# One-hot rows per tile, a copy moved to ScalarE, and other steps reordered in a fused attention and mixture-of-experts kernel

## The chip, the cores and the metric

One core of a Trainium2 chip runs the whole kernel. The metric is the device time of one execution in microseconds, as the median of several runs; before the change it is 367.67 us (three runs, 366.77 to 367.95).

The engines appear in the profile as PE (TensorE, with PEld for its weight loads), DVE (VectorE), ACT (ScalarE), POOL (GpSimd) and SP (SyncE, which only issues transfers here). L12 is line 12 of the kernel before.

## The reference

Attention without softmax, with an RMS norm over each head, and then a layer of eight experts in which each token goes to one expert or to none.

```python
# q, k, v: (8, 8, 576, 64); g_norm: (64,)
kv  = np.einsum('bhsd,bhse->bhde', k, v)
out = np.einsum('bhsd,bhde->bhse', q, kv)
rms = np.sqrt(np.mean(out * out, axis=-1, keepdims=True) + 1e-06)
attn = out / rms * g_norm
x = attn.transpose(0, 2, 1, 3).reshape(4608, 512)

do = x @ w_skip > 0                        # tokens that are computed
logits = x[do] @ w_gate                    # 8 experts
e_idx = argmax(logits); p = softmax(logits)[e_idx]
y = p * (relu(x[do] @ w1[e_idx]) @ w2[e_idx])     # w1[e]: 512x1024, w2[e]: 1024x512
out = x;  out[do] = x[do] + y
```

## The kernel before

The kernel writes its instructions in an order set by hand; each engine runs its own list in that order, and semaphores join them. It has an attention part (to about 107 us) and an experts' part.

**The attention part** runs over 36 units. A unit is 256 tokens' worth of rows for four heads: `units` lists a batch, one of its two blocks of columns, and a half of the heads (`u`). Eight batches in two groups of four make 4 times 8 units and, after each group, two units that gather the rows left over (with `i` None). The main loop (`for n in range(NU + 2)`) writes one step per unit:

- `turn(n + 1)`: four TensorE transposes of q for the next unit (L460), and a ScalarE copy, `qT` (L463).
- `root(n - 1)`: ScalarE's square root of the sums of squares (L529).
- `jobs(n, "early")`, then `values(n)`: for the first two units of a batch two more transposes into the same bank (`turn_8`, L479), four products of qT with k^T v (L498; L508 for the left-over rows), and ScalarE's Square, `sq` (L514). The results go to one of two `o_ps` banks; units 30 and 33 (`THIRDS`) use the bank `sum_ps` instead. A bank is free again when `xl` of its unit is made.
- `jobs(n, "mid")`, `squares(n)` (VectorE's sums `rs`, L522), `norm(n - 1)` (reciprocal L536 and `xl`, L545), `jobs(n, "pe")`; up to step `THIRD + 1` (29) `squares` stands behind `norm`, later ahead of it.
- `finish` and `scale`: GpSimd adds up the gate logits (`lp`, `lg`) and multiplies by the norm's gains (`xb`, L615), which then goes out. `xb` is held back until VectorE's next reciprocal.

**k^T v** of the batches ahead is summed between the units' products (`state`, L383, into `sum_ps`), following the table `portions`. When a batch is done, ScalarE copies the sums to `both` (L390); VectorE copies two quarters of it across partitions into `kvd` (`other`, L394) and GpSimd two more (`own`, L395). `state_t` turns it (L400, copy L402), and `state_m` multiplies by the gate's weights (L408) with four small ScalarE copies into `kvd` (L412). `kvT_ps`, `lg_ps` and the ranks lie side by side in one bank, `g_ps`.

**The tokens' numbering** goes in three groups of 12, 10 and 14 tiles of 128 tokens (`ends`). For each group a stream of small VectorE jobs is written, 2 or 4 to a step (`PACE`): `choose` (the expert of each token, one-hot as `ohb`), `rank` (L696 to L702: running counts by matmul, on top of `top`), `number` (L713 to L728: the slot of each token, split into `hi_k` and `lo_i`, and `oha_k`, for each tile a 128x128 one-hot of its `lo_i`). After the second group `rank_experts` sorts the experts by their counts and SP reads the order; then `early` sends for the first expert's first tokens: `hits` and `bv`, 22 matmuls with `oha_k` (`put`, L924), sums (`rows`, L928), and an indirect gather on GpSimd (L917); `put_more` (L934) does the same for 64 more. `first_in` transposes those tokens (L848) at the "pe" places of steps 33 and 34.

**SP's queue** issues q, k and v (L118), each in four parts, and the stores of `xb` (L653), in the order of the steps.

**The experts' part** (from L1172 on) takes one expert after another, with TensorE's products on sums of blocks (L1252).

## Time and profile before

| | |
|---|---|
| median of three runs | 367.67 us |
| the profiled execution | 366.29 us |
| its span, first to last instruction | 364.4 us |
| TensorE busy, granted clock | 96%, 0.994 |
| 80 to 100 us: PE / DVE / ACT / POOL busy | 17.67 / 18.14 / 13.18 / 14.76 of 20 us |
| 100 to 120 us: the same | 19.23 / 17.69 / 12.27 / 12.82 of 20 us |

A profile's row has its start in us from the span's start, its length, engine, line, operation, what it writes and reads, shapes, and in brackets how long the engine was idle just before and what released it. Consecutive rows of one line are merged, with their count. Starts of successive rows on an engine tell its pace better than lengths, since the end of one operation overlaps the start of the next. Of transfers the profile gives issue and landing.

### The profile page before, as it was taken

The page shows a single profiled execution, that of the slowest core. Times are in us where ns is not written, and L with a number is a line of the kernel's source. Part 1 is how long each engine was busy: PE and PEld are TensorE (multiplying, and loading weights), DVE is VectorE, ACT ScalarE, POOL GpSimd, SP SyncE. Part 2 cuts the span into 40 slices and gives each one's busy share as a digit, 9 for nine tenths or more (in the row PEclk, how much of TensorE's full clock was granted, in tenths as well). Part 3 has the DMA queues.
Part 4 walks back from the last instruction along what each step waited for, and adds up shares of the span by engine and source line. Part 5 has one row for each costly group of instructions (what it writes and reads, how often), then busy time and mean ns, then how long its engine had stood idle before and what let it go on. Part 6 is the DMA issues. An engine that isn't in the chain of part 4 may idle for free.

```text
span 364.4 us, 9568 instructions
## 1 busy us (share of the span) xinstructions
PE 349.5 (96%) x3754; PEld 305.5 (84%) x3754; DVE 249.2 (68%) x637; ACT 145.1 (40%) x418; POOL 125.7 (34%) x205
## 2 busy tenths in 40 slices
PE   8979998999899999999999999999999999999994
PEld 4769987888779669599879978989988998989983
DVE  2545677889888563876937676786776776878831
ACT  2537775676666244244104402512421530431420
POOL 8036777677776072123041102303203203002003
PEclk9989999999999999999999999999999999999999
DMA  8999999999797369873535537455563762601001
GB/s 272 387 390 377 371 392 398 394 394 384 247 335 255 104 208 379 340 262 89 209 107 205 171 124 254 121 224 176 175 230 98 250 235 53 243 1 58 3 2 54
DMA packets 32808, 81.70 MB, mean 224 GB/s; under 512 B 3242, under 2 KB 3250, under 8 KB 32756
## 3 DMA queue, kind: packets, MB, share of 16 engines
q1 hardware_dynamic: 28944, 69.48, 53.7%
q0 software_dynamic: 3792, 11.53, 9.3%
q8 instruction: 31, 0.51, 0.5%
q14 instruction: 21, 0.17, 0.1%
q10 hardware_dynamic: 20, 0.02, 0.0%
HBM read 66.80 MB, written 14.48 MB: 223 GB/s over the span
## 4 chain that ended last, share of the span: by engine, by line
PE 79%; issue 6%; DMA 5%; DVE 5%; POOL 2%; ACT 2%; SPq 0%; POOLq 0%; DVEq 0%; ACTq 0%
PE bank L1252 46%; PE bank L1184 9%; PE o_ps L498 6%; PE sum_ps L383 4%; PE bank L1172 3%; PE q_ps L460 3%; DMA v<-in_v_dram 2%; PE bank L1153 2%; DVE xl L545 1%; DMA xg<-out_dram,src 1%; PE g_ps L859 1%; DMA xg<-out_dram,asrc 1%; PE q_ps L859 1%; PE o_ps L479 1%; DVE rs L522 1%
## 5 line engine op out<-in xcount | busy, mean ns | idle before, releaser
L1262 ACT COPY p<-bank 128x128 f32<-128x128 f32 (+6 forms) x70 | 20.8, 297 | 96.1 <-PE bank L1252 94.6
L1252 PE MATMUL bank<-xt,w 128*128 128x128 f32 (+5 forms) x336 | 55.4, 288 | 0.1
L1383 POOL DMA_INDIRECT out_dram<-xg,rows x14 | 13.9, 996 | 116.2 <-DVE xg L1380 113.0
L1252 PEld LDWEIGHTS bank<-xt,w 128*128 128x128 f32 x336 | 47.0, 190 | 1.9 <-DVE bank L1256 1.4
L615 POOL TENSOR_TENSOR xb<-xl,g_b 128x512 f32<-128x512 f32 x34 | 41.3, 1216 | 18.1 <-DVE rs L536 16.1
L1256 DVE TENSOR_TENSOR bank<-bank,p 128x128 f32<-128x128 f32 (+6 forms) x70 | 23.6, 337 | 29.7 <-PE bank L1252 28.7
L498 PE MATMUL o_ps<-kvd,qT 128*128 128x146 f32 x240 | 36.0, 293 | 1.3 <-DVE xl L545 1.0
L1252 PE MATMUL bank<-xs,s 128*128 128x128 f32 (+5 forms) x224 | 36.7, 288 | 0.0
L498 PEld LDWEIGHTS o_ps<-kvd,qT 128*128 128x128 f32 x240 | 32.1, 192 | 2.1 <-DVE xl L545 1.8
L1252 PEld LDWEIGHTS bank<-xs,s 128*128 128x128 f32 x224 | 31.1, 190 | 1.0 <-ACT p L1262 0.8
L1184 PE MATMUL bank<-w,ht 128*32 128x128 f32 (+2 forms) x424 | 29.9, 313 | 0.0
L522 DVE TENSOR_REDUCE rs<-sq 128x8 f32<-128x512 f32 x36 | 24.5, 681 | 5.4 <-ACT sq L514 5.2
L545 DVE TENSOR_TENSOR xl<-o_ps,rs 128x584 f32<-128x584 f32 x32 | 24.5, 767 | 4.3 <-DVE rs L536 0.5
L1184 PEld LDWEIGHTS bank<-w,ht 128*32 128x32 f32 (+2 forms) x424 | 18.2, 119 | 10.6 <-issue 7.2
L1252 PE MATMUL bank<-t,ht 128*128 128x256 f32 x112 | 27.0, 384 | 0.0
L1252 PE MATMUL bank<-w,ht 128*128 128x256 f32 x112 | 26.5, 380 | 0.0
L383 PE MATMUL sum_ps<-v,k 64*64 64x64 f32 x1152 | 23.5, 223 | 3.0 <-issue 2.6
L1144 POOL DMA_INDIRECT xg<-out_dram,src x14 | 14.3, 1024 | 34.8 <-DMA out_dram<-xg,rows 18.0
L514 ACT ACTIVATE sq<-o_ps 128x512 f32<-128x512 f32 x34 | 20.3, 596 | 14.1 <-PE o_ps L498 13.2
L383 PEld LDWEIGHTS sum_ps<-v,k 64*64 64x64 f32 x1152 | 19.6, 134 | 7.1 <-issue 3.9
L1252 PE MATMUL bank<-t,hs 128*128 128x256 f32 x112 | 25.3, 379 | 0.0
L1252 PEld LDWEIGHTS bank<-t,ht 128*128 128x128 f32 x112 | 20.8, 190 | 3.9 <-issue 1.2
(216 smaller groups left out, 665.2 us busy)
## 6 DMA issues: line engine op xcount, KB each, us to landing
w<-in_moe_w_dram SPq DMA_DIRECT2D x16, 2048.0 KB, 9.0
k<-in_k_dram SPq DMA_DIRECT2D x32, 288.0 KB, 6.0
v<-in_v_dram SPq DMA_DIRECT2D x32, 288.0 KB, 6.3
q<-in_q_dram SPq DMA_DIRECT2D x32, 288.0 KB, 6.2
out_dram<-xb SPq DMA_DIRECT2D x29, 256.0 KB, 6.1
out_dram<-xb POOLq DMA_DIRECT2D x7, 256.0 KB, 6.4
xg<-out_dram,src POOLq DMA_INDIRECT x16, 3.6
out_dram<-xg,rows POOLq DMA_INDIRECT x16, 6.1
```

What stands on the lines that cost most here:

```text
L383: nc.tensor.matmul(out=sum_ps[w * 64:(w + 1) * 64, a, u, :], lhsT=kt[r, 2 * u + w, c, :], rhs=vt[r, 2 * u + w, c, :], start=(c == 0), stop ...
L498: mm = nc.tensor.matmul(out=ps[:, w, 0:2 * PK].rearrange("p (r k) -> p r k", r=2)[:, :, cols], lhsT=qT[:, w, a, :], rhs=kvds[b % KVD][:, w ...
L514: nc.scalar.activation(out=sq[:, :, :, :], in_=heads(ps, G, G + 2 * D), func=ACT.Square)
L522: nc.vector.tensor_reduce(out=rs[:, :, :], in_=sq[:, :, :, :].rearrange("p x y (a d) -> p x (y a) d", a=2), axis=AX.X, op=ALU.add)
L545: nc.vector.tensor_tensor(out=xl[:, :, :, :].rearrange("p x y (a k) -> p x (y a) k", a=2), in0=ps[:, :, 0:2 * PK].rearrange("p x (h k) -> ...
L615: late.append((lambda eng: eng.tensor_tensor(out=xb[:, :, 4 * u * D:(4 * u + 4) * D].rearrange("p r (w x) -> p r w x", w=2), in0=xl[:, :, ...
L1144: nc.gpsimd.indirect_dma_start(out=x_of(xg, off, m), out_offset=None, in_=cut_rows(m)[:, :], in_offset=bass.IndirectOffsetOnAxis(ap=idx[:, ...
L1184: nc.tensor.matmul(out=yps[q * m:(q + 1) * m, 0:n], lhsT=ht(f)[:, off:off + m], rhs=w_sb[r][1][:, f, q * n:(q + 1) * n], start=(f == 0), s ...
L1252: nc.tensor.matmul(out=out, lhsT=lhsT(i), rhs=rhs(i), start=start and i == 0, stop=i == k - 1, skip_group_check=True)
L1256: nc.vector.tensor_tensor(out=to, in0=x, in1=y, op=ALU.add)
L1262: nc.scalar.copy(out=t, in_=x)
L1383: ins = nc.gpsimd.indirect_dma_start(out=cut_rows(m)[:, :], out_offset=bass.IndirectOffsetOnAxis(ap=rows[:, col:col + 1], axis=0), in_=x, ...
```

## The change

Six edits:

- `oha_k` is made one tile at a time, by a TENSOR_SCALAR that compares a two-byte row of the numbers 0 to 127 (`row128`) with that tile's `lo`, a per-partition scalar; before, one TENSOR_TENSOR on whole numbers made two tiles (or seven in the last group). `lo` comes from `hi_k` by a multiply and add, in place of a bitwise and.
- For the batches from 5 on (`ACROSS`), ScalarE makes the two copies of k^T v across partitions, one ahead of `values` and one behind it, in place of VectorE.
- `rank` moves from the place "pe" to "mid"; `state_m` of batches 4 and 6 (`RANKED`) moves to "early" of the next step.
- `rank_experts` does without three small operations: `kbase` is made once in the setup, and the order is summed straight to whole numbers.
- In `early`, the sums and both gathers (`put_rows`) move behind `squares`; the transposes of the unit after next are written ahead of them.
- The step from which `squares` stands ahead of `norm` is `THIRD + 1` in place of `THIRD + 2`.

```diff
-    row128_i = keep.tile([P, P], I32)
+    row128_i = att_pool.tile([P, P], I32, tag="sq", name="row128_i", bufs=2)
     nc.gpsimd.iota(row128_i[:, :], pattern=[[1, P]], base=0, channel_multiplier=0)
+    row128 = keep.tile([P, P], BF16)
...
+    nc.vector.tensor_copy(out=row128[:, :], in_=row128_i[:, :])
...
+    kbase = keep.tile([P, E], FP32)
+    nc.vector.scalar_tensor_tensor(out=kbase[:, :], in0=ebase[:, :], scalar=-float(E),
+                                   in1=eorder[:, :], op0=ALU.mult, op1=ALU.add)
...
         for w in range(2):
-            nc.vector.tensor_copy(out=other(b, w)[:, :, cols], in_=both[w * 64:(w + 1) * 64, :, :])
+            if b < ACROSS:
+                nc.vector.tensor_copy(out=other(b, w)[:, :, cols], in_=both[w * 64:(w + 1) * 64, :, :])
             nc.gpsimd.tensor_copy(out=own(b, w)[:, :, cols], in_=both[w * 64:(w + 1) * 64, :, :])
 
+    def state_across(b, w):
+        if b >= ACROSS:
+            nc.scalar.copy(out=other(b, w)[:, :, G:G + 2 * D], in_=boths[b][w * 64:(w + 1) * 64, :, :])
...
-        lo_i = gat_pool.tile([P, TG], I32, tag="lo_i", name="lo_i")[:, 0:nt]
-        nc.vector.tensor_single_scalar(out=lo_i, in_=s_i, scalar=127, op=ALU.bitwise_and)
-        yield
         nc.vector.tensor_single_scalar(out=hi_k[:, t0:t1], in_=s_i, scalar=7,
                                        op=ALU.arith_shift_right)
         yield
+        lo = gat_pool.tile([P, TG], FP32, tag="lo", name="lo")[:, 0:nt]
+        nc.vector.scalar_tensor_tensor(out=lo, in0=hi_k[:, t0:t1], scalar=-128.0, in1=s_i,
+                                       op0=ALU.mult, op1=ALU.add)
+        yield
         step = 2 if g < LAST else nt // 2
         for t in range(0, nt, step):
-            nc.vector.tensor_tensor(out=oha_k[:, t0 + t:t0 + t + step, :],
-                                    in0=row128_i[:, :].unsqueeze(1).to_broadcast([P, step, P]),
-                                    in1=lo_i[:, t:t + step].unsqueeze(2).to_broadcast([P, step, P]),
-                                    op=ALU.is_equal)
+            for i in range(t, t + step):
+                nc.vector.tensor_scalar(out=oha_k[:, t0 + i, :], in0=row128[:, :],
+                                        scalar1=lo[:, i:i + 1], scalar2=None, op0=ALU.is_equal)
             yield
...
-        key = count_tokens("key", gat_pool)
-        nc.vector.scalar_tensor_tensor(out=key[:, :], in0=key[:, :], scalar=float(E),
-                                       in1=eorder[:, :], op0=ALU.mult, op1=ALU.add)
+        key = gat_pool.tile([P, E], FP32, tag="key", name="key")
+        nc.vector.scalar_tensor_tensor(out=key[:, :], in0=top[:, :], scalar=float(E),
+                                       in1=kbase[:, :], op0=ALU.mult, op1=ALU.add)
...
-        nc.vector.tensor_reduce(out=order_f[:, :], in_=gt[:, :, :], axis=AX.X, op=ALU.add)
-        yield
-        nc.vector.tensor_copy(out=order_i[:, :], in_=order_f[0:1, :])
+        with nc.allow_low_precision(reason="whole numbers"):
+            nc.vector.tensor_reduce(out=order_i[:, :], in_=gt[:, :, :], axis=AX.X, op=ALU.add)
...
-            rows = gat_pool.tile([P, 2], FP32, tag="rows1", name="rows1")
-            nc.vector.tensor_reduce(out=rows[:, :], in_=ps.rearrange("p (c i) -> p c i", i=2),
-                                    axis=AX.X, op=ALU.add)
-            gather(rows[:, 0:1], P, 0)
-
-            def put_more():
+            turn(now[0] + 2)
+            turned_ahead.append(now[0] + 2)
+
+            def put_rows():
+                rows = gat_pool.tile([P, 2], FP32, tag="rows1", name="rows1")
+                nc.vector.tensor_reduce(out=rows[:, :], in_=ps.rearrange("p (c i) -> p c i", i=2),
+                                        axis=AX.X, op=ALU.add)
+                gather(rows[:, 0:1], P, 0)
                 more = g_ps[:, GB + 4:GB + 5]
...
                 gather(more, 64, P)
-            at(now[0], "pe", put_more)
+            assert now[0] > THIRD
+            at(now[0], "squared", put_rows)
...
+    RANKED = (4, 6)
...
-            at(step, "pe", lambda b=b: state_m(b))
+            for w, part in enumerate(("early", "mid")):
+                at(step, part, lambda b=b, w=w: state_across(b, w))
+            at(step + (b in RANKED), "early" if b in RANKED else "pe", lambda b=b: state_m(b))
...
-        yield lambda: rank(g)
+        yield "mid", lambda: rank(g)
...
-        if 1 <= n < NU - 1:
+        if 1 <= n < NU - 1 and n + 1 not in turned_ahead:
             turn(n + 1)
...
-        if THIRD + 2 <= n < NU:
+        if THIRD < n < NU:
             squares(n)
+        jobs(n, "squared")
         done = norm(n - 1) if 1 <= n <= NU else None
-        if n < THIRD + 2:
+        if n <= THIRD:
             squares(n)
```

What this moves, at three places. The line numbers of the changed kernel are higher by 5 to 10.

TensorE around the second ranking, before: the products of unit 24 (`kvd_161`), `state_m` of batch 6 (L408), a part of batch 7's sums (L383), then the ranking, whose first row is L696.

```order
L498 MATMUL o_ps<-kvd_161,qT 128x2x73 x4
L408 MATMUL g_ps<-gw_b,kvT 128x36 x2
L383 MATMUL sum_ps<-v,k 64x64 x16
L696 MATMUL g_ps<-top,ident 128x88
L699 LDWEIGHTS ut
```

The same place in the changed kernel, and, behind the ranking's rows, what follows up to unit 25's products:

```order
L508 MATMUL o_ps<-kvd_163,qT 128x2x73 x4
L706 MATMUL g_ps<-top,ident 128x88
L709 LDWEIGHTS ut
...
L712 MATMUL g_ps<-ohb,ones 128x8
L388 MATMUL sum_ps<-v,k 64x64 x16
L470 MATMUL q_ps<-ident,q 128x2x64 x4
L418 MATMUL g_ps<-gw_b,kvT 128x36 x2
L508 MATMUL o_ps<-kvd_163,qT 128x2x73 x4
```

The ranking now follows the products directly, and `state_m` (now L418) stands behind the transposes of unit 26's q (L470), ahead of unit 25's products.

TensorE around the placing for the first gather, before: unit 29's products, unit 31's transposes, unit 30 (`sum_ps`), the 22 placing matmuls (L924), and the one that waits for their sums (L934).

```order
L498 MATMUL o_ps<-kvd_164,qT 128x2x73 x4
L460 MATMUL q_ps<-ident,q 128x2x64 x4
L479 MATMUL sum_ps<-ident,q 128x128 x2
L498 MATMUL sum_ps<-kvd_167,qT 128x2x73 x4
L924 LDWEIGHTS oha_k
...
L934 MATMUL g_ps<-rows_2044,again_64_243 128x1
L460 MATMUL q_ps<-ident,q 128x2x64 x4
```

In the changed kernel:

```order
L508 MATMUL o_ps<-kvd_166,qT 128x2x73 x4
L932 LDWEIGHTS oha_k
...
L470 MATMUL q_ps<-ident,q 128x2x64 x4
L944 MATMUL g_ps<-rows_2039,again_64_247 128x1
L489 MATMUL sum_ps<-ident,q 128x128 x2
L508 MATMUL sum_ps<-kvd_169,qT 128x2x73 x4
L470 MATMUL q_ps<-ident,q 128x2x64 x4
```

The placing comes one unit sooner, unit 31's transposes stand between it and the matmul on its sums (now L944), and unit 30's products stand behind that matmul.

VectorE between the sums of unit 27 and the first gather's rows, before: each group of L536, L545, L522 is the reciprocal and `xl` of one unit and the sums of the next.

```order
L522 TENSOR_REDUCE rs<-sq 128x8
L728 TENSOR_TENSOR oha_k<-row_i,lo_i 128x256 x3
L899 TENSOR_TENSOR ohc_1975<-hi_k,colid_i 128x44
L536 RECIPROCAL rs<-rs 128x8
L545 TENSOR_TENSOR xl<-o_ps,rs 128x584
L522 TENSOR_REDUCE rs<-sq 128x8
L904 TENSOR_TENSOR bv_2002<-ohc_1975,row_k 128x88
L928 TENSOR_REDUCE rows_2044<-g_ps 128x2
```

In the changed kernel:

```order
L532 TENSOR_REDUCE rs<-sq 128x8
L740 TENSOR_SCALAR oha_k<-row_138,lo 128x128 x4
L907 TENSOR_TENSOR ohc_1987<-hi_k,colid_i 128x44
L912 TENSOR_TENSOR bv_1989<-ohc_1987,row_k 128x88
L532 TENSOR_REDUCE rs<-sq 128x8
L940 TENSOR_REDUCE rows_2039<-g_ps 128x2
```

`bv`, which the placing waits for, no longer stands behind the reciprocal and `xl` of unit 28; these come behind the gathers' rows. Ahead of this piece the two copies of L394 are gone, and six one-hots stand in place of two instructions of two tiles each.

11 lines of the change are left out of this document (5 added, 6 removed).

## The prediction

> **What bounds the kernel now.** I read the page first (busy shares), then the time by windows, then TensorE's timeline with its waits, and last the VectorE, SP and ScalarE rows around the places where TensorE waits.
>
> ```profile
> PE 349.5 (96%) x3754; PEld 305.5 (84%) x3754; DVE 249.2 (68%) x637; ACT 145.1 (40%) x418; POOL 125.7 (34%) x205
> ...
> 75.00:90.00 15.00, 14.34 (x303) 12.89 (x301) 12.79 (x36) 9.75 (x25) 10.22 (x19) 1.00 1.04 388
> ...
> 140.00:340.00 200.00, 199.96 (x1568) 179.23 (x1567) 142.83 (x344) 61.92 (x186) 36.36 (x39) 1.00 0.52 176
> ```
>
> The columns after the first two are PE, PEld, DVE, ACT, POOL, the granted clock, the DMA share and GB/s. From 140 to 340 us TensorE has no idle time that matters, and the change touches nothing there. So whatever the change is worth is the time by which TensorE gets sooner through the attention part, up to the first expert's input. There these are its waits (start, length, what released it):
>
> ```profile
> 62.05 0.47 PE L696 MATMUL g_ps<-top,ident 128*128 128x104 f32 x2 [0.96 <-ACT kvd L412]
> ...
> 84.40 0.46 PE L696 MATMUL g_ps<-top,ident 128*128 128x88 f32 x2 [0.45 <-ACT kvd L412]
> 96.19 1.26 PE L498 MATMUL o_ps<-kvd,qT 128*128 128x146 f32 x8 [1.02 <-DVE xl L545]
> 99.75 0.69 PE L924 MATMUL g_ps<-bv,oha_k 128*128 128x4 bf16 x22 [0.65 <-DVE bv L904]
> 100.70 0.38 PE L934 MATMUL g_ps<-rows,again 128*128 128x1 f32 x2 [0.25 <-DVE rows L928]
> 104.53 0.81 PE L171 MATMUL q_ps<-ones 128*128 128x512 bf16 x3 [0.31 <-ACT qT L463]
> 106.69 0.63 PE L848 MATMUL q_ps<-ident,xg 128*128 128x128 f32 x4 [0.20 <-DMA xg<-out_dram,src]
> ```
>
> They sum to 3.84 us: 1.41 at the two rankings, 2.43 between 95 and 107, where VectorE sets the pace. From 106.69 on TensorE runs on without a listed wait until 131. Were all of this gone the kernel would gain 3.8 us, and that is the ceiling. All estimates below are of the start of that row at 106.69 (the first expert's transposes).
>
> **The change part by part.** *Ranks ahead of gates.* The ranking waited for L412, four ScalarE copies that themselves wait for state_m's matmul (L408). Now the ranking goes ahead of L408, so the 0.96 and 0.45 go. What is late next: L408 now stands in the following step, ahead of that step's values, and reads as waiting for VectorE's `pr` and `top`. At the first ranking I put the gain at 0.6 us, the 0.96 less about 0.35 for that new wait; it lasts through the next units, since no wait of over 0.2 stands on TensorE between 66 and 84 us. But then:
>
> ```profile
> 78.73 0.98 SPq L118 DMA_DIRECT2D q<-in_q_dram  x1
> ...
> DMA to landing us min/median/max: 6.2/6.2/6.2
> ...
> 85.00 0.63 PE L460 MATMUL q_ps<-ident,q 128*128 128x128 f32 x4
> 85.47 1.16 PE L498 MATMUL o_ps<-kvd,qT 128*128 128x146 f32 x8
> ```
>
> The landing line is that of the single issue at 78.73, the second quarter of batch 6's q: it lands at 84.9 to 85.0, and the third and fourth transposes of L460 at 85.00 read it. TensorE arrives there with nearly no slack. The DMA share is 1.04 from 75 to 90 us at 388 GB/s; the queue is full, the bytes ahead of this q are the same after the change, so I take its landing as fixed. **Both rankings' gains therefore end in a wait at this q.** The last two transposes take half of 85.47-85.00, so they end at 85.2; now L408 follows (0.39, from 94.14 to 94.53 below) ahead of the values: unit 25's values start at 85.6 instead of 85.47. Net of this part: 0.1 us *later*. (Bounds: 0.4 later, if a store of GpSimd's that comes sooner takes the queue from this q; 1.05 sooner, 0.6 + 0.45, if the q comes sooner with the rest.)
>
> *From 85.6 to unit 29.* TensorE's own pace is read from these rows:
>
> ```profile
> 87.90 1.16 PE L498 MATMUL o_ps<-kvd,qT 128*128 128x146 f32 x8
> ...
> 90.44 1.16 PE L498 MATMUL o_ps<-kvd,qT 128*128 128x146 f32 x8
> ...
> 93.14 1.16 PE L498 MATMUL o_ps<-kvd,qT 128*128 128x146 f32 x8
> 94.14 0.56 PE L408 MATMUL g_ps<-gw_b,kvT 128*128 128x36 f32 x4
> 94.53 0.63 PE L460 MATMUL q_ps<-ident,q 128*128 128x128 f32 x4
> ...
> 97.94 1.16 PE L498 MATMUL sum_ps<-kvd,qT 128*128 128x146 f32 x8
> ```
>
> Units 26, 27, 28 start at 87.90, 90.44, 93.14, steps of 2.43, 2.54 and 2.70 without a wait; after the change 88.0, 90.6, 93.3. Unit 29 then needs 1.00 (values) + 0.39 (L408) + 0.47 (L460) = 1.86, so TensorE is ready at 95.2, and waits for VectorE's `xl` of unit 27. VectorE:
>
> ```profile
> 9.87 0.38 DVE L266 TENSOR_SCALAR row_i<-row_i,upper 128x32 int32<-128x32 int32 x2
> ...
> 92.33 0.69 DVE L522 TENSOR_REDUCE rs<-sq 128x8 f32<-128x512 f32 x1
> 93.04 0.69 DVE L394 COPY kvd<-both 64x256 f32<-64x256 f32 x2
> ...
> 94.06 1.06 DVE L728 TENSOR_TENSOR oha_k<-row_i,lo_i 128x256 bf16<-128x256 int32 x2
> 95.04 0.19 DVE L536 RECIPROCAL rs<-rs 128x8 f32<-128x8 f32 x1
> 95.37 0.77 DVE L545 TENSOR_TENSOR xl<-o_ps,rs 128x584 f32<-128x584 f32 x1
> 96.05 0.68 DVE L522 TENSOR_REDUCE rs<-sq 128x8 f32<-128x512 f32 x1
> 96.64 1.18 DVE L728 TENSOR_TENSOR oha_k<-row_i,lo_i 128x256 bf16<-128x256 int32 x3
> 97.74 0.19 DVE L899 TENSOR_TENSOR ohc<-hi_k,colid_i 128x44 bf16<-128x44 int32 x1
> ```
>
> *One-hot rows.* Five instructions for ten tiles took 95.04-94.06 = 0.98 and 97.74-96.64 = 1.10, 0.21 a tile. The new form is a TENSOR_SCALAR with a per-partition scalar, on 128 two-byte elements. The trace has that kind at L266: two in 0.38; the last one's tail runs beside what follows, 1.18 - 1.10 = 0.08 in the rows at 96.64, so (0.38 - 0.08) / 2 = 0.15 from one to the next at 32 elements. I take **0.17 each** (1.7 for ten, 0.4 saved), near that row. Bounds: 0.10, half of the 0.21 that a tile takes now; and 0.27, if the 96 elements more go by at the rate of `xl` (584 in 96.05-95.37 = 0.68, 0.12 for 96), 0.6 lost. Splitting them costs the fixed part twice as often, which eats most of what the narrower rows save. [...]
>
> *k^T v across on ScalarE.* L394 goes, 0.69 us on VectorE at 93.04 for batch 7 (and for 5 and 6 ahead of the q wait, where it buys nothing). ScalarE gets two copies around its Square:
>
> ```profile
> L1262 ACT COPY p<-bank 128x128 f32<-128x128 f32 (+6 forms) x70 | 20.8, 297 | 96.1 <-PE bank L1252 94.6
> ...
> L514 ACT ACTIVATE sq<-o_ps 128x512 f32<-128x512 f32 x34 | 20.3, 596 | 14.1 <-PE o_ps L498 13.2
> ```
>
> 0.30 for 128 elements and 0.60 for 512 put one of 256 at 0.4 (bounds 0.3 and 0.6). They delay L412, the next qT and the next Square by 0.4 to 0.8, and VectorE still has one-hots to make in that time; where it has not, the delay is a new wait (counted below).
>
> So `xl` of unit 27: its squares are ready 1.9 after its values (92.33-90.44), 92.5; rs 0.6; `lo` 0.2; six one-hots 1.0; reciprocal 0.3; `xl` 0.77: ends at 95.4. Unit 29 starts at **95.4 instead of 96.19**.
>
> *Sums beside the placing, one step sooner.* With one operation less in the numbering and in the order of the experts, the placing (L924) falls into step 29 instead of 30. rs of 28 ends at 96.0, four one-hots 0.7, ohc and bv 0.4: the placing starts at 97.2, not 99.75. The rest of the chain:
>
> ```profile
> 100.48 0.16 DVE L928 TENSOR_REDUCE rows<-g_ps 128x2 f32<-128x4 f32 x1 [0.79 <-PE g_ps L924]
> ...
> 104.41 0.77 DVE L545 TENSOR_TENSOR xl<-sum_ps,rs 128x584 f32<-128x584 f32 x1
> ...
> 105.23 1.26 PE L498 MATMUL sum_ps<-kvd,qT 128*128 128x146 f32 x8
> ...
> 101.37 5.18 DMA xg<-out_dram,src
> ```
>
> rs of 29 now comes ahead of `rows`, and its Square stands on ScalarE behind the copies: ready at 97.6, rs to 98.2, `rows` at 98.3, and 0.89 behind it (101.37-100.48) the first gather leaves: 99.2, some 2.2 us sooner. But unit 30's values now stand behind L934, which waits for `rows`: 99.0 instead of 97.94. Behind it: Square 100.75, rs 101.35, reciprocal and `xl` of 29 to 102.4; ohc 0.4, rs 0.6, reciprocal and `xl` of 30 to 104.5, where it ended at 105.2. Unit 33 reuses that bank and starts at 104.55 instead of 105.23. 1.26 later, without the 0.20 for the gather (99.2 + 5.2 = 104.4), the expert's transposes start at **105.8 instead of 106.69: 0.9 us sooner**, most of it the 0.7 of VectorE's shorter list.
>
> *The rest.* The cast of the row numbers and `kbase` fall into the setup, beside VectorE's 5.1 us wait; about 0.2 us each, and hidden:
>
> ```profile
> L235 DVE TENSOR_SCALAR gw_b<-o_ps,gcol 64x36 f32<-64x36 f32 x2 | 0.5, 255 | 5.1 <-ACT g_b L229 5.1
> 122.85 0.39 DVE L820 TENSOR_TENSOR srow<-srow,g_ps 128x24 f32<-128x24 f32 x2 [1.13 <-PE g_ps L762]
> ```
>
> The last group's fourteen one-hots, 2.4 in place of two instructions, come 0.4 later; VectorE stands idle for 1.13 behind them, so they are covered.
>
> Sum: 366.29 (the profiled execution; span 364.4 and 1.9 around it) - 0.9 = 365.4. The runs' median, 367.67, is 1.38 above that execution; the forecast on it is **366.8 us**.
>
> **Rivals.** *(1) The q does not hold it.* If batch 6's q comes as much sooner as TensorE does, unit 25 starts at 85.47 - 0.6 - 0.45 = 84.4, 1.2 before the forecast's 85.6. VectorE would give back 0.3 of it: 0.9 + 0.9 = 1.8 in all, **365.9**. For it: a part of SP's issues waits on other engines. Against: the DMA share of 1.04.
>
> *(2) Nothing comes through.* VectorE's saving is used up by new waits: unit 30 behind L934, the Square behind the copies, the gather among the first expert's weights (it is sent while that 2 MB load is on the queue; landing 1 us later than 104.4 + the 1.3 of slack costs the rest). **367.6.** For it: my forecast has 1.2 us of fresh waits on VectorE between 97 and 103 already.
>
> *(3) Slower: the one-hots and GpSimd hold each other up.* The trace shows such a thing where L394 runs beside GpSimd's copies of the same tile:
>
> ```profile
> L394 DVE COPY kvd<-both x10: 288/410/452, 47.2 to 93.4; 64x256 f32<-64x256 f32 x10
> ...
> 93.58 0.87 POOL L395 COPY kvd<-both 64x256 f32<-64x256 f32 x2
> ...
> L615 POOL TENSOR_TENSOR xb<-xl,g_b 128x512 f32<-128x512 f32 x34 | 41.3, 1216 | 18.1 <-DVE rs L536 16.1 <-DVE ohb L685 1.9
> ```
>
> (The first row's numbers are the shortest, median and longest, in ns.) The copies of L394 spread from 0.29 to 0.45. The one-hots start when rs ends, 1.6 us (96.64-95.04) after the reciprocal that releases GpSimd's `xb` of 1.2. If `xb` starts over 0.4 late it is still running then, and if a one-hot has to stand until it ends, that is up to 1.2 for each of two groups, 2.0 of it not covered, which turns 0.9 sooner into 1.1 later: **368.8**. Against: the old one-hots at 94.06, beside the row at 93.58, took 0.49 each against 0.37 at 96.64, a loss of 0.1 and not of a whole operation. [...]
>
> **How the numbers follow.** Forecast 0.52, rival 1 0.17, rival 2 0.21, rival 3 0.10. 0.3%, 1.1 us, is about what a measurement of this kernel tells from no change; the forecast's own range is 0.4 to 1.4 sooner (0.10 or 0.27 for a one-hot, the q 0.3 either way), and 0.20 of its 0.52 lie over 1.1. Faster 0.20 + 0.17 = 0.37; slower 0.10; the same 0.53. The range takes in rival 1 and rival 2 with the runs' spread of half a microsecond: 365.5 to 368.1.
>
> **What would show it.** The transposes of unit 26 waiting for the q; no L696 wait on L412; one-hots 0.17 apart; the placing near 97 and the first gather near 99; unit 30's values at 99; the expert's transposes at 105.8. The forecast is wrong if the q lands before 84.5, or if GpSimd rows overlap the one-hots and these stand over 0.3 apart.

## The result and the profile after

The changed kernel is **slower**: a median of 372.51 us over six executions (369.88 to 373.67) beside 367.80 for the kernel before (366.77 to 368.39, six executions). The ratio is 1.0125, with a 95% interval of 1.0085 to 1.0165. The profiled execution of the changed kernel took 373.67 us, its span 371.9, 7.5 more than the 364.4 of before.

From the page of the changed kernel, the sums by engine and the clock in 40 slices:

```profile
PE 353.6 (95%) x3754; PEld 308.9 (83%) x3754; DVE 249.7 (67%) x654; ACT 147.8 (40%) x424; POOL 126.7 (34%) x205
...
PEclk9989999899989999999999999999999999999998
```

Its time by windows (from:to and length, busy time of PE, PEld, DVE, ACT and POOL, then the granted clock, the DMA share and GB/s):

```profile
66.00:70.00 4.00, 3.43 (x34) 3.24 (x35) 1.43 (x5) 0.94 (x3) 1.18 (x3) 0.57 1.05 359
...
104.00:107.00 3.00, 3.00 (x14) 2.99 (x14) 1.32 (x5) 1.24 (x4) 2.33 (x3) 0.50 1.04 418
...
140.00:340.00 200.00, 199.97 (x1580) 178.86 (x1577) 139.15 (x333) 60.60 (x180) 40.08 (x42) 1.00 0.54 186
```

From 140 us on nothing has changed: TensorE is as full as before. Ahead of it the clock now falls to one half three times (the first three 8s in the PEclk line; the last 8 is the end, where TensorE has no more work); before, once, near 25 us. The second of the three lies in the first window, at 0.57, and the third in the second, at 0.50. TensorE's timeline (start, duration, engine, line, operation, tiles, and in brackets the idle time ahead and what ended it; "issue" stands where the profile shows nothing that the engine waited for, called a wait without a releaser below):

```profile
62.09 0.47 PE L706 MATMUL g_ps<-top,ident 128*128 128x104 f32 x2
...
64.03 0.64 PE L418 MATMUL g_ps<-gw_b,kvT 128*128 128x36 f32 x4 [0.59 <-DVE top L724]
...
66.57 0.91 PE L388 MATMUL sum_ps<-v,k 64*64 64x64 f32 x21 [1.03 <-issue]
...
86.62 0.35 PE L706 MATMUL g_ps<-top,ident 128*128 128x88 f32 x2
...
99.73 1.26 PE L508 MATMUL o_ps<-kvd,qT 128*128 128x146 f32 x8 [0.60 <-DVE xl L555]
102.42 0.71 PE L932 MATMUL g_ps<-bv,oha_k 128*128 128x4 bf16 x22 [1.43 <-DVE bv L912]
...
111.92 0.60 PE L856 MATMUL q_ps<-ident,xg 128*128 128x128 f32 x4
...
115.42 0.74 PE L518 MATMUL o_ps<-kvd,q 64*64 64x73 f32 x32 [0.78 <-DVE xl L555]
...
138.15 0.66 PE L1168 MATMUL bank<-ident,xg 128*128 128x128 f32 x4 [1.06 <-DMA xg<-out_dram,asrc]
```

The rankings (62.09, 86.62) wait no more, and the wait at unit 29 is 0.60 in place of 1.02. In their place stand 0.59 at `state_m`, 1.43 at the placing in place of 0.65, 0.78 at 115.42 (unit 35) and 1.06 at the second expert's tokens (L1168). Before, the first half of these tokens stood ready and the second half waited 0.22:

```profile
130.75 0.60 PE L1153 MATMUL bank<-ident,xg 128*128 128x128 f32 x4
131.58 0.33 PE L1153 MATMUL bank<-ident,xg 128*128 128x128 f32 x1 [0.22 <-DMA xg<-out_dram,asrc]
```

One execution of one kernel differs from the next by a microsecond or two. So the comparison goes by stages, from the start of one TensorE row to the start of another (us). The last column is the spread over all 19 profiles of this study, and says which stages the change reaches. Units 25 to 28 (7.67 and 8.22) are left out:

| Stage on TensorE | before | changed | over all profiles |
|---|---|---|---|
| start to unit 16 | 59.84 | 61.47 | 58.4 to 61.5, either order of code |
| unit 16 to 17 (first ranking) | 3.49 | 3.12 | 3.48 or 3.49 with the old order, 3.11 or 3.12 with the new; once 4.47 |
| unit 17 to 20 | 7.74 | 10.02 | 7.7 to 10.1, either |
| unit 20 to 24 | 10.73 | 11.01 | 10.6 to 10.8; 11.0 with ScalarE's three copies |
| unit 24 to 25 (second ranking) | 3.68 | 3.26 | 3.7; 3.25 to 3.4 with the new order; 4.1 to 4.5 where a q, `ohb` or (in `old_rank`) ScalarE's copies were late |
| unit 28 to 29 | 3.05 | 2.62 | 3.05 to 3.4; with ScalarE's copies 2.6, or 2.2 with the old one-hots |
| unit 29 to the first layer's second part (the 16 matmuls of L859, now L867, that begin with 64 columns) | 13.74 | 16.37 | 13.4 to 14.7; 15.4 to 16.7 with the early placing |
| from there to the second expert's transposes (L1153, now L1168) | 20.83 | 22.06 | 20.8 to 21.0; 21.1 to 22.4 with fourteen one-hots; 22.2 in `before_shift` and `rank_across_xb` |
| from these to their second run | 12.36 | 12.45 | 11.9 to 14.3, either |
| from the second run of those transposes to the end | 221.28 | 221.30 | 221.2 to 221.8 |

So the change gains 0.37 + 0.42 + 0.43, loses 0.3 in units 20 to 24, and then loses 2.6 around the placing (a stretch at half clock among it) and 1.2 behind it. The rest of the 7.5 us lies ahead of unit 16 (1.6), in units 17 to 20 (2.3) and in units 25 to 28 (0.6): late loads, waits without a releaser, the wait at `state_m` and a half clock.

### The profile page after: what moved, and what is told of

Same layout as the page of the kernel before. It is cut to its first block, busy times and chain, and to the rows that moved or that the text cites. A ratio compares the mean times of both kernels' runs of the same rounds, so it can differ in the third digit from the quotient of the medians.

```text
span 371.9 us, 9585 instructions
## 1 busy us (share of the span) xinstructions
PE 353.6 (95%) x3754; PEld 308.9 (83%) x3754; DVE 249.7 (67%) x654; ACT 147.8 (40%) x424; POOL 126.7 (34%) x205
## 4 chain that ended last, share of the span: by engine, by line
PE 77%; issue 7%; DVE 7%; DMA 3%; ACT 3%; POOL 2%; SPq 0%; DVEq 0%; POOLq 0%; ACTq 0%
PE bank L1267 45%; PE bank L1199 8%; PE o_ps L508 6%; PE sum_ps L388 4%; PE bank L1187 3%; PE q_ps L470 3%; DMA v<-in_v_dram 2%; DVE xl L555 2%; PE bank L1168 2%; DVE rs L532 2%; DMA xg<-out_dram,asrc 1%; PE o_ps L489 1%; PE g_ps L418 1%; PE q_ps L867 1%; PE g_ps L867 1%
## 5 line engine op out<-in xcount | busy, mean ns | idle before, releaser
L1277 ACT COPY p<-bank 128x128 f32<-128x128 f32 (+6 forms) x70 | 20.8, 297 | 96.1 <-PE bank L1267 94.7
L508 PEld LDWEIGHTS o_ps<-kvd,qT 128*128 128x128 f32 x240 | 32.9, 197 | 1.7 <-DVE xl L555 1.2
L388 PE MATMUL sum_ps<-v,k 64*64 64x64 f32 x1152 | 25.1, 225 | 5.5 <-issue 4.5
L388 PEld LDWEIGHTS sum_ps<-v,k 64*64 64x64 f32 x1152 | 20.6, 136 | 10.1 <-issue 7.0
L1199 PEld LDWEIGHTS bank<-w,ht 128*32 128x32 f32 (+2 forms) x424 | 18.2, 119 | 10.6 <-issue 7.2
L1159 POOL DMA_INDIRECT xg<-out_dram,src x14 | 14.3, 1025 | 35.0 <-DMA out_dram<-xg,rows 18.9
L473 ACT COPY qT<-q_ps 128x512 f32<-128x512 f32 x32 | 18.8, 586 | 14.3 <-PE q_ps L470 13.9
```

Source lines behind the costliest of these rows:

```text
L388: nc.tensor.matmul(out=sum_ps[w * 64:(w + 1) * 64, a, u, :], lhsT=kt[r, 2 * u + w, c, :], rhs=vt[r, 2 * u + w, c, :], start=(c == 0), stop ...
L473: nc.scalar.copy(out=qT[:, :, :, :].rearrange("p w a t -> p (w a t)"), in_=ps[:, :, :, :, :].rearrange("p w a h t -> p (w a h t)"))
L508: mm = nc.tensor.matmul(out=ps[:, w, 0:2 * PK].rearrange("p (r k) -> p r k", r=2)[:, :, cols], lhsT=qT[:, w, a, :], rhs=kvds[b % KVD][:, w ...
L1159: nc.gpsimd.indirect_dma_start(out=x_of(xg, off, m), out_offset=None, in_=cut_rows(m)[:, :], in_offset=bass.IndirectOffsetOnAxis(ap=idx[:, ...
L1199: nc.tensor.matmul(out=yps[q * m:(q + 1) * m, 0:n], lhsT=ht(f)[:, off:off + m], rhs=w_sb[r][1][:, f, q * n:(q + 1) * n], start=(f == 0), s ...
L1277: nc.scalar.copy(out=t, in_=x)
```

## The experiments

Seventeen runs follow, of the two kernels and of fifteen others, each beside the kernel before on the same chip. Ratios are to that kernel; the chip differs from one group of runs to the next, so small differences between their ratios or profiles say little.

**1. Is it the change or the execution?** Both kernels, unchanged.

> The kernel before, unchanged, for a second profile. Theory A (the change itself makes TensorE wait, at the state multiplication behind the ranking near 64 us and at the placing near 101 us, and each wait of over 1.2 us is followed by 3.4 us at half the clock): this profile shows no stretch at half clock but the one at 25 us, and its waits at L383 are those of the first profile. Theory B (the loads and the code of TensorE come late in some executions, whatever the kernel): waits of about 0.9 us at L383 with no releaser, or a v that lands 0.7 us later in the first 20 us, appear here too, and the span is 366 us or more.

> The changed kernel, unchanged. Theory A: 1.01 to 1.015 again; the placing waits 1.2 to 1.5 us for bv, held by one ohc of 1.2 us beside GpSimd's xb, and the clock halves behind it; L418 waits 0.5 to 0.6 for VectorE at 64 us. Theory B: the late v of the first 20 us (0.7) and the two waits of L388 without a releaser (0.88 at 45, 1.03 at 66 us) are gone or elsewhere, and the span is at most 368.

Before: 370.72 us in one execution (before's others on that chip had a median of 369.15), no half clock at all, yet waits at L383 without a releaser of up to 1.4 and one of 1.0 us at a later placing (L762); so theory A's half clock behind each wait of over 1.2 us does not hold. After: 371.78, ratio 1.0101 [1.0044, 1.0158]; the placing waits 1.29, but no half clock follows it. So the waits without a releaser belong to the execution (theory B is right on them), and those at `state_m` (0.59 again), the placing and unit 35 (0.79) belong to the change. The second expert's tokens wait 0.22 here, as before, and its stage is 21.11: most of the 1.2 lost there does not come with every execution. The placing was held by another instruction than theory A said: `ohc` takes 0.19, and `bv` behind it 1.11 in place of 0.24.

```profile
98.52 0.19 DVE L907 TENSOR_TENSOR ohc<-hi_k,colid_i 128x44 bf16<-128x44 int32 x1
98.75 1.11 DVE L912 TENSOR_TENSOR bv<-ohc,row_k 128x88 bf16<-128x88 bf16 x1
```

**2. The placing at its old place** (`late_put`): the changed kernel with the sums and gathers behind the placing as before, and a step later.

```diff
-            turn(now[0] + 2)
-            turned_ahead.append(now[0] + 2)
-            def put_rows(): ...
+            rows = ...; gather(rows[:, 0:1], P, 0)
+            def put_more(): ...
-        if THIRD < n < NU:
+        if THIRD + 2 <= n < NU:
         if g == LAST - 1:
+            yield
             yield from early()
```

> The changed kernel with the placing back at its old place, one step later and behind unit 30's products, and the sums and gathers behind it as before. Theory A: the wait ahead of the placing falls from 1.4 to 0.7 us or less and no half clock follows it: 2 to 2.5 us faster than the changed kernel, ratio to before 1.004 to 1.008. Theory B: within 0.5 us of the changed kernel.

Ratio 1.0034 [1.0010, 1.0058]: by the medians two thirds of the 1.0% are gone, and no half clock follows the placing. TensorE's timeline there:

```profile
97.62 1.16 PE L508 MATMUL sum_ps<-kvd,qT 128*128 128x146 f32 x8
99.12 0.69 PE L932 MATMUL g_ps<-bv,oha_k 128*128 128x4 bf16 x22 [0.34 <-DVE bv L912]
...
107.11 0.63 PE L856 MATMUL q_ps<-ident,xg 128*128 128x128 f32 x4 [1.24 <-DMA xg<-out_dram,src]
```

With unit 30's products (97.62) between unit 29's and the placing, the wait falls to 0.34. But a new one of 1.24 shows at the first expert's tokens: what was gained ahead of it is lost there.

**3. The early placing alone** (`early_only`): the kernel before with the order of the experts in fewer steps, the early placing, and the sums beside it, and nothing else. (That order loses two operations and one step, and the numbering loses none; the list of the change counts three operations, and the prediction one for the numbering too.)

```diff
 (the changed kernel)
-    RANKED = (4, 6)
+    RANKED = ()
-        yield "mid", lambda: rank(g)
+        yield lambda: rank(g)
-    kvTs, boths, ACROSS = {}, {}, 5
+    kvTs, boths, ACROSS = {}, {}, 8
 (and the one-hots of before)
```

> The kernel before with one part of the change: the order of the experts in fewer steps, the placing one step sooner and the sums and gathers beside it; one-hots, rankings and copies as before. Theory A (this part costs most): 1.5 to 1.8 us from unit 29's products to the first layer's second part beside what the earlier gather gives back (13.7 to 14.5 before, 15.4 to 15.6 here), ratio 1.004 to 1.008. Rival (it costs only together with the late one-hots): 1.000 to 1.002.

Ratio 1.0080 [1.0049, 1.0110]. From unit 29 to the first layer's second part it is 16.67 us. TensorE's timeline, and the window behind the placing:

```profile
97.22 1.26 PE L506 MATMUL o_ps<-kvd,qT 128*128 128x146 f32 x8 [1.35 <-DVE xl L553]
99.86 0.71 PE L930 MATMUL g_ps<-bv,oha_k 128*128 128x4 bf16 x22 [1.39 <-DVE bv L910]
...
101.73 2.15 PE L506 MATMUL sum_ps<-kvd,qT 128*128 128x146 f32 x8
```

```profile
101.00:104.00 3.00, 3.00 (x15) 2.99 (x15) 1.43 (x6) 0.80 (x3) 2.19 (x3) 0.50 1.04 419
```

The products at 101.73 take 2.15 in place of 1.16: the clock has halved behind the wait. So this part alone costs most of what the changed kernel loses, and with the old one-hots too. That the clock halves because of the wait is read from the order of the two (more on it in the last section).

**4. Is it the instruction that GpSimd holds?** In the changed kernel, the timelines of VectorE and of GpSimd ahead of the placing:

```profile
97.08 1.58 DVE L740 TENSOR_SCALAR oha_k<-row,lo 128x128 bf16<-128x128 bf16 x6
...
100.18 0.78 DVE L740 TENSOR_SCALAR oha_k<-row,lo 128x128 bf16<-128x128 bf16 x4
100.88 1.19 DVE L907 TENSOR_TENSOR ohc<-hi_k,colid_i 128x44 bf16<-128x44 int32 x1
102.11 0.25 DVE L912 TENSOR_TENSOR bv<-ohc,row_k 128x88 bf16<-128x88 bf16 x1
```

```profile
100.84 1.18 POOL L625 TENSOR_TENSOR xb<-xl,g_b 128x512 f32<-128x512 f32 x1
```

`ohc` took 0.19 before (97.74 there) and takes 1.19 now: it starts 0.04 after GpSimd's `xb` and ends with it. `put` itself sends that `xb` (`scale`). In each of the six profiles with the early placing `ohc`, `bv` or a comparison behind them (L752) stands like this beside an `xb`; up to 112 us none does in the thirteen others. In `xb_later` the first `xb` goes behind the gathers.

```diff
         def put():
-            scale(now[0])
             for t in range(NE):
```

> The changed kernel, with GpSimd's xb that runs beside ohc (from 100.84 to 102.02) moved behind the two gathers and held until VectorE's next reciprocal. Theory A1 (GpSimd holds VectorE's ohc for its whole operation): ohc takes 0.2 in place of 1.19 us, the placing starts 1.0 sooner behind unit 29's products and waits 0.3 to 0.5 us instead of 1.3 to 1.4, the first gather leaves 1.0 to 2.0 sooner; the ratio to before falls from 1.010 to 1.004 to 1.007. Rival (the wait is there because no products stand between unit 29's and the placing, and ohc only happens to lie in it): ohc stays at 1.2 or another instruction takes its place, and the placing waits 1.3 as before, ratio 1.010.

Ratio 1.0111 [1.0076, 1.0146], no better than the changed kernel. Its timelines of VectorE and of TensorE:

```profile
98.15 0.19 DVE L907 TENSOR_TENSOR ohc<-hi_k,colid_i 128x44 bf16<-128x44 int32 x1
...
103.64 1.99 DVE L752 TENSOR_TENSOR ohc<-colid_i,hi_k 128x264 bf16<-128x264 int32 x1
```

```profile
98.68 0.71 PE L931 MATMUL g_ps<-bv,oha_k 128*128 128x4 bf16 x22 [0.42 <-DVE bv L912]
...
107.29 1.26 PE L508 MATMUL sum_ps<-kvd,qT 128*128 128x146 f32 x8 [1.60 <-DVE xl L555]
```

`ohc` is free (0.19) and the placing waits 0.42, as theory A1 has it. But now another comparison (L752, 0.43 before) runs into two later `xb` in a row (102.81 to 104.00 and 104.16 to 105.33) and takes 1.99, and unit 33 waits 1.60 for the `xl` behind it. The stage is 15.56 us, as in `after_again` (15.43). So the hold is real, and taking it away at one instruction moved it to the next: the rival's outcome, by A1's mechanism. No run took every hold away, so how much of the stage's loss is holds, and how much the placing's place ahead of unit 30's products alone, is not shown.

**5. TensorE kept busy while it waits** (`fill`): `dense(5, ...)` ahead of the placing.

> The changed kernel with five idle matmuls (128x512, on ones, into a free bank) ahead of the placing, some 1.1 us, so that TensorE is busy while it waits for bv. Nothing else waits for them. Theory A2 (a wait of 1.3 us makes the clock halve for 3.4 us in some executions): no half clock between 100 and 110 us, the ratio falls by 0.002 to 0.004 on the average of the runs, from 1.010 to 1.006 to 1.008, and the runs spread less. Rival (the half clock does not come from this wait): ratio 1.009 to 1.012, spread as before.

Ratio 1.0083 [1.0052, 1.0114]; four executions took 369.18 to 371.67, one 374.97. That is less than 1.0101 and 1.0111, inside their intervals, and the stage is 15.40, as in `after_again`: this run doesn't decide. No half clock stood there in its profile, but in `after_again` none did either.

**6. The rankings** (`old_rank`: the changed kernel with `RANKED = ()` and `rank` at "pe"; `rank_only` and `rank_across`: the kernel before with the new rankings, without and with ScalarE's copies).

> The changed kernel with the rankings and the state multiplication of batches 4 and 6 back at their old places. Theory A: the 0.6 us wait of L418 goes, the ranking waits 1.0 for ScalarE again, and the half clock at 66 us goes: 1 to 2 us faster than the changed kernel, ratio 1.007 to 1.011. Theory B: the waits at L388 near 45 and 66 us stay as they are; the time stays within 0.5 us of the changed kernel, or is 0.5 to 1 us longer since the rankings wait again.

> The kernel before with one part of the change: the rankings ahead of the state multiplication, and that of batches 4 and 6 one step later. By the four profiles of the changed orders the first ranking gives 0.4 us and the second 0.4 by unit 26, and VectorE's wait at unit 29 (1.0 us) takes back most of it: ratio 0.997 to 1.000. Rival (late loads or code hold TensorE there, and the rest of the loss comes from this part): 1.002 to 1.005.

> The kernel before with two parts of the change: the rankings, and ScalarE's copies of k^T v for batches 5 to 7; one-hot rows, placing and order of the experts as before. The wait at unit 29 falls from 1.0 to 0.6 or less, as in all profiles of the change: ratio 0.996 to 0.999. Rival (what is left of the loss in the version with the late placing, 1.003, comes from these two parts and not from the one-hot rows): 1.002 to 1.005.

`old_rank` 1.0090 [1.0034, 1.0147]: the rankings wait again (0.96 and 0.83), and a half clock falls behind the first (unit 16 to 17 takes 4.47). Theory A's gain of 1 to 2 us didn't come: the ratio lies in its range, but the median, 372.29, is no better than the changed kernel's 371.78 on that chip. `rank_only` 1.0040 [1.0016, 1.0064], in the rival's range: the second ranking now waits 0.58 for `ohb`, since VectorE makes that behind its copies of k^T v; `rank_across` 1.0006 [0.9988, 1.0024], without that wait and with 0.19 at unit 29, a ratio between the two that were expected. Rankings and copies belong together, and together they give nothing that can be measured.

**7. The fourteen one-hots** (`late_two_last`: `late_put` with the last group in two instructions; `hots_only`: the kernel before with the new one-hots).

```diff
+            if g == LAST:
+                nc.vector.tensor_tensor(out=oha_k[:, t0 + t:t0 + t + step, :], ...)
+                yield
+                continue
             for i in range(t, t + step):
```

> The version with the late placing, with the last group's fourteen one-hots made by two instructions again (seven tiles each, as before, but on the two-byte row). Theory C (the fourteen one-hots end 0.5 us later, and the last xb behind them on VectorE, its store and the second expert's gather with them; where the store then meets a block of TensorE's code on a DMA engine, 1.2 us more): from the first layer's second part (the 16 matmuls L867 of 64 columns) to the transposes of the second expert's tokens it is 20.8 to 20.9 us, as in all four profiles with the old form, against 21.1 to 22.4 with the new; the ratio falls from 1.0034 to 0.999 to 1.002. Rival (the rest of the loss is in front of the placing, or in the rankings): 21.1 to 22.4 again and ratio 1.003 to 1.005.

> The kernel before with one part of the change: the one-hot rows tile by tile. Theory C: the stretch from the first layer's second part to the second expert's transposes grows from 20.8 to 21.1 to 22.4, ten one-hots ahead of the placing take 2.1 to 2.3 us as before (0.25 each beside GpSimd's copies, 0.17 without), so nothing is won there: ratio 1.002 to 1.004. My own prediction's step (0.4 us saved by the ten, the last group covered): 0.998 to 1.000.

The stage is 20.83 in `late_two_last` and 22.27 in `hots_only`, as theory C has it, and `hots_only` is at 1.0060 [1.0029, 1.0092], more than was expected. But `late_two_last` stays at 1.0033 [1.0015, 1.0051]: the ratio was a miss. TensorE's timeline shows where the stage's gain went:

```profile
133.33 0.66 PE L1173 MATMUL bank<-ident,xg 128*128 128x128 f32 x4
135.44 0.33 PE L1173 MATMUL bank<-ident,xg 128*128 128x128 f32 x1 [1.45 <-DMA xg<-out_dram,asrc]
```

The stage ends at 133.33, and the second half of the same tokens waits 1.45 right behind it: their gather landed 4.15 us behind its issue, where it took 3.12 in the kernel before. The next stage takes 13.65 in place of 12.36. `late_first_reg` below has the same (4.12, a wait of 1.33, 13.53). Why this gather is late in that form no run shows. VectorE's timeline in the kernel before and in the changed one:

```profile
117.03 2.09 DVE L728 TENSOR_TENSOR oha_k<-row_i,lo_i 128x896 bf16<-128x896 int32 x2
...
120.43 1.28 DVE L615 TENSOR_TENSOR xb<-xl,g_b 128x512 f32<-128x512 f32 x2
```

```profile
123.43 2.38 DVE L740 TENSOR_SCALAR oha_k<-row,lo 128x128 bf16<-128x128 bf16 x14
...
127.10 1.29 DVE L625 TENSOR_TENSOR xb<-xl,g_b 128x512 f32<-128x512 f32 x2
```

Reckoned from `pr` (115.77 and 121.94), `xb` starts 4.66 and 5.16 behind: 0.5 later. Its store goes out behind it, and the second expert's gather leaves 1.1 to 1.2 us behind that store's landing (before: landed at 125.90, gather at 127.05; changed: 133.55 and 134.70).

**8. Where the other 1.2 us come from.** A 16 KB block of code (the queue that the page calls "q8 instruction", 31 packets, 0.51 MB) is fetched near there, in 0.93 us. I take it for TensorE's: from 14 to 125 us one comes for every 240 or so of its instructions on the mean (91 to 321 between two in the kernel before). `before_shift` moves it, with twelve tiny matmuls that nobody reads; `hots_shift` moves it away from the store in `hots_only`, with forty.

```diff
+    def tiny(count):
+        for _ in range(count):
+            nc.tensor.matmul(out=g_ps[:, GB:GB + 4], lhsT=ones[:, :], rhs=ones[:, 0:4], ...)
         def put():
             scale(now[0])
+            tiny(12)
```

> The kernel before with twelve tiny matmuls (four columns each) ahead of the placing, where TensorE waits 0.65 us anyway; they shift every later 16 KB block of TensorE's code by 24 instructions, so the block of 125.4 us is fetched about 1 to 1.5 us sooner, while the last store of xb is on the DMA engines. Theory C (the block holds the store up): the store lands 4.3 to 4.8 us behind its issue instead of 3.3 to 3.5, and the stretch from the first layer's second part to the second expert's transposes grows from 20.83 to 21.5 to 22.2. Rival (the block does not matter): 20.8 to 20.9. The ratio is 1.001 to 1.004, or 1.000.

> The kernel before with the one-hot rows tile by tile, and 40 tiny matmuls ahead of unit 29's products and of the placing, so that the block of code is fetched some 2.5 us sooner, ahead of the store. Theory C: the store lands 3.2 to 3.6 us behind its issue instead of 4.46, and the same stretch falls from 22.27 to 21.0 to 21.4 (what is left is the 0.5 us of the one-hots themselves). Rival: 22.0 to 22.4 as without the matmuls.

The store's landing, by the DMA line of its two issues, first in the kernel before, then in `before_shift`, `hots_only` and `hots_shift` (shortest, median, longest; the longest is the second issue):

```profile
DMA to landing us min/median/max: 3.2/3.3/3.5
```

```profile
DMA to landing us min/median/max: 3.7/4.4/5.0
```

```profile
DMA to landing us min/median/max: 3.4/3.9/4.5
```

```profile
DMA to landing us min/median/max: 3.4/3.6/3.8
```

Moving the block made the store of the old kernel land at 5.0 and its stage grow from 20.83 to 22.19; moving it in the new form brought the landing from 4.5 to 3.8 and the stage from 22.27 to 21.62. Theory C holds, though 5.0, 3.8 and 21.62 each lie a little above what was expected. The other profiles bear it out: in six the block starts 2.0 to 2.6 us behind the store's second issue, and the store lands 4.4 to 5.0 behind that issue; in ten it starts 2.9 to 3.1 behind, and the store lands at 3.3 to 3.6. (Ratios 1.0041 [1.0016, 1.0065] and 1.0026 [1.0003, 1.0050].)

**9. VectorE's last `xb` ahead of the numbering** (`rank_across_xb`: `scale(NU, eng=nc.vector)` ahead of `drain(number(LAST))`).

> The kernel before with the rankings and ScalarE's copies, and VectorE's last xb moved ahead of the last group's numbering, so that its store has 2.5 us of slack. A try at a version that beats both. If the store sets the second expert's gather, the gather leaves about 2 us sooner and its wait of 0.2 us goes, and no code block can hold it: ratio 0.997 to 1.000 (1.0006 without the move). If the last group's placing is late instead, VectorE's placing input comes 1.3 later and TensorE waits there: 1.001 to 1.003.

1.0050 [1.0024, 1.0076]: the second case, and worse than its range. The last placing waits 1.2 for VectorE.

**10. Why the early gains come to nothing** (`first_reg`: `rank_across`, and SP reads the first expert's number alone ahead of its weights; `late_first_reg`: the same in `late_two_last`).

```diff
         for r in range(E):
             experts_of.append(nc.values_load(order_i[0:1, r:r + 1], ...))
+            if r == 0:
+                load_weights(0, wpool_a, later=True)
...
-            load_weights(0, wpool_a, later=True)
```

> The kernel before with the rankings and ScalarE's copies (1.0006 [0.9988, 1.0024]), and SP reading the first expert's number alone before it sends for that expert's weights; the other seven reads follow. Theory D (the first gather lands when the 2 MB of weights ahead of it on the DMA engines are through, and these leave when SP has read the order; so what the attention part gains sooner ends in a wait for that gather, 0.94 us there): the weights leave some 2 us sooner, the wait for the gather goes, and the time from unit 29's products to the first layer's second part falls from 14.63 to 13.4 to 13.8; ratio 0.996 to 0.999. Rival (the gather's landing follows its own issue): wait and ratio stay, 1.000.

> The changed kernel with the late placing, the last group in two instructions (1.0033 [1.0015, 1.0051]), and the first expert's number read alone before its weights are sent for. Theory D: no wait for the first gather, 13.3 to 13.8 us from unit 29's products to the first layer's second part; ratio 0.997 to 1.001. If the rest of this version's 0.3% is not in the stages at all but in more waits for code or half clocks, it stays at 1.001 to 1.004 though each stage is as short as before.

Three rows of the timeline, the weights' issue, the first gather's, and TensorE's first transposes, in `rank_across` and then in `first_reg`:

```profile
93.00 0.42 SPq L337 DMA_DIRECT2D w<-in_moe_w_dram  x1
...
100.84 1.09 POOL L922 DMA_INDIRECT xg<-out_dram,src  x1 [0.63 <-DVE src L920]
...
106.90 0.63 PE L853 MATMUL q_ps<-ident,xg 128*128 128x128 f32 x4 [0.94 <-DMA xg<-out_dram,src]
```

```profile
90.55 0.42 SPq L337 DMA_DIRECT2D w<-in_moe_w_dram  x1
...
100.93 1.09 POOL L924 DMA_INDIRECT xg<-out_dram,src  x1 [0.63 <-DVE src L922]
...
105.90 0.60 PE L855 MATMUL q_ps<-ident,xg 128*128 128x128 f32 x4
```

The gathers leave at the same time (100.84, 100.93); with the weights 2.45 us sooner the gather lands 3.93 behind its issue in place of 5.93, the wait of 0.94 is gone and TensorE goes on at 105.90. So the first gather's landing follows the weights ahead of it, and is not a fixed time behind its own issue. The ratios: 0.9997 [0.9972, 1.0021], a little above what was expected, and 0.9996 [0.9975, 1.0018]; the second was 1.0033 without this edit, on another chip.

**11. A version that is faster than both** (`six_up`: `first_reg`, with VectorE still copying batch 5: `ACROSS = 6`).

> The version with rankings, ScalarE's copies and the first expert's number read alone (0.9997 [0.9972, 1.0021]), with VectorE still copying batch 5's k^T v and ScalarE only that of batches 6 and 7. In every profile with all three batches on ScalarE, units 20 to 24 took 11.03 us in place of 10.73 (10.63 in others), by a wait of 0.2 us for xl at a transpose of unit 22. Theory E (that is batch 5's copy, delaying Square): 10.6 to 10.8 us here, the rest of the stages as in first_reg, ratio 0.996 to 0.999, the fastest of all. Rival: 11.0 as before and ratio 0.999 to 1.001.

Ratio **0.9958** [0.9938, 0.9978], on one chip. Units 20 to 24 take 10.62 us; the wait that batch 5's copy had put ahead of a transpose is gone, as TensorE's timeline shows (first `rank_across`, then `six_up`):

```profile
75.88 0.44 PE L484 MATMUL o_ps<-ident,q 128*128 128x128 f32 x2 [0.21 <-DVE xl L550]
```

```profile
78.25 0.41 PE L484 MATMUL o_ps<-ident,q 128*128 128x128 f32 x2
```

The stage gives 0.4 us; between 0.9997 and 0.9958 lie 1.4. So theory E accounts for a part of the gain alone, and the rest is not explained; `first_reg` ran on another chip.

## Why the prediction was wrong

- **Where the change acts** (the attention part only, the rest equal): right; from the second expert's later transposes to the end all profiles agree within 0.6 us.
- **Ranks ahead of gates**: the mechanism was right, the size near. The first gave 0.37 (forecast 0.6), since `state_m` waits 0.59 for `top` and not 0.35. The second gave 0.42. That batch 6's q would take both back was right only where TensorE came early enough: in `rank_across` and `xb_later` it waited there for q, in the changed kernel's own profiles it came after the q, having been held up before.
- **One-hots**: 0.17 each was right where nothing disturbs: the four at 100.18 stand 0.70 in all. (In the kernel before, the old form took 0.18 a tile at 96.64, 1.10 for six, and `top`, a COPY of 8 elements at 115.97, 0.15. By that, which is an estimate, most of a one-hot's time is fixed.) Beside GpSimd's copies of k^T v the six at 97.08 took 1.50, 0.25 each, so ten took 2.20 against 2.08 in the old form. The saving of 0.4 was a loss of 0.1, and more by the stage: unit 29 came 3.24 behind unit 28 in `hots_only`, in place of 3.05, and 2.62 in place of 2.22 beside ScalarE's copies.
- **k^T v on ScalarE**: unit 29 was to come 2.1 behind unit 28 (93.3 and 95.4), in place of 3.05; it came 2.62 behind, with the old one-hots 2.22. The 0.3 that the copies cost in units 20 to 24 was not in the sum: I had said that VectorE has other work in that time, and at unit 22 TensorE waited for its `xl`.
- **Sums beside the placing, a step sooner: the step that failed.** I put unit 29 to the first expert's transposes at 10.4 us, 0.1 less than before. It was 11.25 in `after_again` and 12.19 in the first profile. I had seen that unit 30 now stands behind the placing and its sums, but not what the placing's wait becomes with no products ahead of it: I put the placing 1.8 behind the start of unit 29's products (95.4 and 97.2), and it came 2.55 and 2.69 behind, with a wait of 1.3 to 1.4, because `ohc` or `bv` met an `xb` and stood 0.9 to 1.0 longer. I had counted 0.4 for the two together. The 0.7 that I gave VectorE back as its shorter list went to the next comparison that met an `xb` (L752, 0.76 and 1.39 in the changed kernel, 0.43 before). That moving this part costs the time is shown both ways (`late_put`, `early_only`); that the holds are the reason is shown for single waits, not for the whole of the stage.
- **The first gather** was forecast to land 5.2 behind its issue, 2.2 sooner than before. Its landing follows the weights (experiment 10); sending it sooner buys at most the 0.2 to 1.2 us that TensorE would wait.
- **The last group's one-hots covered by an idle of 1.13**: wrong by its neighbour. That idle is behind `xb`, not ahead of it, and `xb` with its store is what the second expert's gather waits for. Price: 0.3 to 1.6 us, the larger part where a block of code meets the store.
- **The half clock** was in no term. The six executions of the changed kernel go with it: 369.88 us at a mean clock of 0.997, 371.23 and 371.83 at 0.988 and 0.989, 373.19 to 373.67 at 0.984. The profiled one, at 0.984, has three stretches of 3.4 us ahead of its end, some 0.005 of the mean each; by that estimate the others have none, two and three. So about 2 us of the loss stand in the one execution without such a stretch, and each stretch goes with about 1 us more. The stages say the same: 4.47 in place of 3.49 in units 16 to 17 (`old_rank`), 16.37 in place of 15.43 behind unit 29.
- **The rivals.** Rival 3 (slower, 368.8, at 0.10) had the mechanism, GpSimd's `xb` holding a VectorE instruction for its whole length, but on the one-hots; it held the comparisons `ohc` and `bv`. I had set against it that the old one-hots beside a GpSimd copy lost 0.1 and not a whole operation; but what counted here is which instructions the new order puts beside an `xb` (`ohc` 1.19 in place of 0.19), and I had looked at the one-hots alone. Rival 2 had unit 30 behind L934 and the weights ahead of the gather; the second is what swallows the early gains.

What stays open: `late_two_last` is 0.3% slower than the kernel before. The late gather of its second half (1.3 us) is of that size, but `late_first_reg` has it too and is at 0.9996. Its profile also shows 6.5 us of waits without a releaser at L388 where the others show 2 to 5; but that was its slowest execution, 370.04 beside a median of 368.29. `first_reg` and `six_up` differ by who copies batch 5's k^T v, and show 0.9997 and 0.9958, so a part of a per cent hangs on things that no run here separates. That a wait brings on the half clock was not proved by taking it away (`fill`); it rests on the rows below.

## What to carry to other kernels

A step that is moved ahead of other work on the engine that waits has that work as cover no longer; count the wait anew, with nothing beside it (here 1.43 us at the placing in place of 0.65). Ask of every short instruction on VectorE in the new order which GpSimd operation it now meets (beside an `xb`, `ohc` took 1.19 us in place of 0.19). And before a gain is summed up, look for the next transfer that doesn't move with it: here the weights ahead of a gather, and one store behind the last item of a list.
